# Retention and feed-forward on one core: q and k loads ahead of the weights on GpSimd, then on SyncE; v loaded as stacked fp32 on SyncE; transposes one unit ahead; 256-token groups at both ends

## The chip, the core and the metric

The kernel runs on one core of one Trainium2 chip. A core has five engines, each with its own instruction queue worked in order: TensorE (PE in the profile, with its weight loads as PEld), VectorE (DVE), ScalarE (ACT), GpSimd (POOL) and SyncE (SP, which here only issues DMAs). Sixteen DMA engines move data between memory and the core; SP, ACT and POOL each feed them through a queue of their own. The metric is the device time of one execution in microseconds, lower is better.

## What is computed

q, k and v have the shape (8 batches, 8 heads, 576 positions, 64). The first half is a decaying, causal linear attention (retention), the second a feed-forward with a leaky ReLU over all 4608 tokens, 512 wide with 2048 hidden.

```python
scores = scale * np.matmul(q, k.transpose(0, 1, 3, 2))
gamma = 1.0 - 2.0 ** (-5.0 - np.arange(H))
Dmat = np.where(rel >= 0, gamma[:, None, None] ** rel, 0.0)
attn = np.matmul(scores * Dmat, v)
x = attn.transpose(0, 2, 1, 3).reshape(B * S, H * D)
h = x @ w_in
out = np.maximum(0.01 * h, h) @ w_out
```

## The kernel before

**Units.** The attention is worked in 40 units: each of the 8 batches has four units of 128 tokens and one, the fifth (`w == 4`), of 64. A unit consists of blocks of 64 tokens. For a unit `u` these steps are written:

- `load(u)` (L127): two DMAs on SyncE bring q and k of the unit as fp32, in pieces of 64 numbers (256 bytes), into a pool of four buffers each (`ld`).
- `load_v(b)` (L110): eight DMAs on GpSimd bring v of a whole batch and turn it to fp16 on the way. Two batches have room.
- `cast(u)` (L142): multiplies q and k by the decay tables and makes them fp16 (`qk16`). q is done on GpSimd, k on VectorE for the first five units and on GpSimd later.
- `st_transpose(u)`: VectorE copies v into block-diagonal weights `vdiag` (L162, two copies) and k into `kstk` (L170, four copies of 64x256; none for the unit of 64 tokens); TensorE makes eight transposes (L177) into the PSUM tile `tr`; ScalarE copies `qT` out of it (L184), and ScalarE and VectorE copy half of `kdiag` each (L186).
- `st_state(u, j)`: four matmuls (L203) add a block's k·v to the running state `ups`; VectorE turns it into fp16 weights `sdiag` (L229 to L233).
- `st_scores(u)`: eight matmuls (L242), then VectorE multiplies by the causal mask (L253).
- `st_out(u)`: matmuls with `vdiag` and `sdiag` (L275, L280) into `ot`; ScalarE copies the result to `xT` (L286), the input of the feed-forward.

**Feed-forward.** 4608 tokens are 9 groups of 512. `g1(g, fc)` is four matmuls of 512 columns with `w_in` (L352) into one of two PSUM buffers `hps`, and the leaky ReLU on ScalarE (L359) into `gt`. `g2(g, n)` is four matmuls with `w_out` (L371) into `yps`; every fourth is followed by a copy on VectorE (L380) and the output DMA on SyncE (L382).

**Order.** Nothing is rescheduled: each engine's queue holds its instructions in the order in which the Python code writes them. The attention of a unit is a list of slots: `s0` (load of unit u+4, `load_v` of the next batch when `w == 1`, `cast(u+2)`, `st_transpose(u)`), then state, scores, state, out. The units of the first 512 tokens (0 to 3) are written first. Then, in loop `g`, the 16 pieces of `g1(g)` alternate with the 16 of `g2(g-1)`, and the attention slots of the next group are spread between them evenly, the last one behind the last piece. Loop 8 and the last `g2` hold no attention.

**Start.** SyncE issues q and k of units 0 to 3. GpSimd issues v of batch 0 (eight DMAs), casts q of units 0 and 1, then issues the weights: four DMAs for `w_in` (L325), each a quarter of the hidden columns, and four for `w_out` (L330), all turned to fp16 on the way.

**Waits of the DMA queues.** Eight semaphores serve GpSimd's DMAs in turn and eight others SyncE's. A DMA that takes a semaphore waits until the DMA eight before it has landed. A load into a pool buffer also waits until the engine that read the buffer's last content is done.

Of the kernel before, what the change touches and what calls it, by code (L numbers as in the profile page):

```python
# [18 lines left out]
def kernel(  # L19
# [20 lines left out]
    P = 128  # L40
# [28 lines left out]
    v_pool = ctx.enter_context(tc.tile_pool(name="vp", bufs=2))  # L69
    a_pool = ctx.enter_context(tc.tile_pool(name="ap", bufs=3))  # L70
# [32 lines left out]
    vst = {}  # L103

    def load_v(b):
        t = v_pool.tile([P, NP, NI, D], F16, name="vst")
        vst[b] = t
        for p in range(NP):
            for hh in range(2):
                nc.gpsimd.dma_start(  # L110
                    out=t[CH * hh : CH * hh + CH, p, :, :],
                    in_=v[b, 2 * p + hh].rearrange("(i s) d -> s i d", s=CH),
                )

# [4 lines left out]
    qk16 = {}  # L119

    def load(u):
        b, w = units[u]
        n = nrows[u]
        for x, t_ap in enumerate((q, k)):
            t = ld_pool.tile([P, H, D], FP, name=f"qk32_{x}")
            qk32[u, x] = t
            nc.sync.dma_start(  # L127
                out=t[0:n],
                in_=t_ap[b, :, P * w : P * w + n, :].rearrange("h t d -> t h d"),
            )  # L130

    def cast(u):
        b, w = units[u]
        n = nrows[u]
        for x in range(2):
# [5 lines left out]
            eng = nc.vector if (u < 5 and x == 1) else nc.gpsimd  # L141
# [5 lines left out]
            )  # L147

# [7 lines left out]
    def st_transpose(u):  # L156
# [4 lines left out]
        for hh in range(2):  # L161
            nc.vector.tensor_copy(  # L162
                out=vdiags[z][CH * hh : CH * hh + CH, :, 0:nb, CH * hh : CH * hh + CH],
                in_=vst[b][CH * hh : CH * hh + CH, :, 2 * w : 2 * w + nb, :],
            )
# [19 lines left out]
        for hh, eng in ((0, nc.scalar.copy), (1, nc.vector.tensor_copy)):  # L185
# [7 lines left out]
    def st_state(u, j):  # L193
# [8 lines left out]
        for p in range(NP):  # L202
# [3 lines left out]
                rhs=vst[b][:, p, i, :],  # L206
# [18 lines left out]
        for hh in range(2):  # L225
# [4 lines left out]
            elif nxt < 3:  # L230
                nc.vector.tensor_copy(out=dst, in_=ut[lo:hi])
# [55 lines left out]

    def slots(u):

        b, w = units[u]  # L290

        def s0():
            if u + 4 < NU:
                load(u + 4)
            if w == 1 and b + 1 < B:
                load_v(b + 1)
            if u + 2 < NU:
                cast(u + 2)
            st_transpose(u)

        yield s0
# [15 lines left out]
    load(0)  # L317
    load_v(0)
    for u in range(1, 4):
        load(u)  # L320
    cast(0)
    cast(1)
# [12 lines left out]
    first_slot = []  # L335
    need = []
    for u in range(NU):
        b, w = units[u]
        lo = b * NI + 2 * w
        for s in slots(u):  # L340
            first_slot.append(s)
            need.append(lo // 8)
    done = 0

    g_tiles = {}

    def g1(g, fc):
        if fc == 0:
            g_tiles[g] = g_pool.tile([P, NF, TOK], F16, name="gt")
        hps = h_pool.tile([P, TOK], FP, name="hps")  # L350
        for c in range(NP):
            nc.tensor.matmul(  # L352
                out=hps,
                lhsT=w_in16[:, c, fc * P : (fc + 1) * P],
                rhs=xT[:, c, g * TOK : (g + 1) * TOK],
                start=(c == 0),
                stop=(c == NP - 1),
            )
        nc.scalar.activation(  # L359
            out=g_tiles[g][:, fc, :], in_=hps,  # L360
            func=mybir.ActivationFunctionType.Lrelu,
        )

    y_cur = {}

    def g2(g, n):
        tb, part = n // 4, n % 4
        if part == 0:
            y_cur[g] = y_pool.tile([P, DM], FP, name="yps")
        for f in range(4 * part, 4 * part + 4):  # L370
            nc.tensor.matmul(  # L371
                out=y_cur[g],
                lhsT=g_tiles[g][:, f, tb * P : (tb + 1) * P],
                rhs=w_out16[:, f, :],
                start=(f == 0),
                stop=(f == NF - 1),
            )
        if part == 3:
            osb = o_pool.tile([P, DM], FP, name="osb")
            nc.vector.tensor_copy(out=osb, in_=y_cur[g])  # L380
            r0 = g * TOK + tb * P
            nc.sync.dma_start(out=out[r0 : r0 + P, :], in_=osb)  # L382

    def run_slots(upto):
        nonlocal done
        while done < upto:
            first_slot[done]()
            done += 1

    total = len(first_slot)  # L390
    ends = [sum(1 for x in need if x <= g) for g in range(NG)] + [total]
    run_slots(ends[0])
    for g in range(NG + 1):
        a = done
        e = ends[min(g + 1, NG)] if g < NG else total
        nblk = (16 if g < NG else 0) + (16 if g > 0 else 0)
        m = 0
        for n in range(NF):
            if g < NG:
                g1(g, n)  # L400
                m += 1
                run_slots(a + (e - a) * m // nblk)
            if g > 0:
                g2(g - 1, n)
                m += 1
                run_slots(a + (e - a) * m // nblk)
# [30 lines left out]
```

## Time and profile before

| what | value |
|---|---|
| median of 3 runs | 366.31 us (366.26 to 366.71) |
| the profiled execution | 366.62 us, of which 364.9 us are the span of the trace |
| granted TensorE clock, mean | 0.994 |
| busy: DVE, ACT, POOL | 198.1, 144.2, 131.4 us |
| DMA, whole span | 37.71 MB in 122479 packets, 113744 of them under 512 B |
| issue to landing, median: q or k of 256 KB; v of 72 KB; `w_in`; `w_out` | 4.3 and 4.4; 5.0; 12.5; 23.3 us |

The page divides the span into 40 slices of 9.1 us and shows in each, in tenths, how busy an engine was. Groups of instructions are listed by line, engine and the tiles they write and read, with count, total busy time, mean duration, and the idle time ahead of them with what ended it. The span begins with the first instruction; 1.7 us of the execution's time (366.62 less 364.9) lie around it.

### The profile page before, as it was taken

The numbers are of one execution on the slowest core, as the hardware profiler recorded it, in microseconds if no ns is written. First come the engines' busy times: TensorE is split into PE (matmuls) and PEld (weight loads), VectorE is DVE, ScalarE is ACT, GpSimd is POOL, SyncE is SP. The second block draws the span as 40 slices with busy tenths as digits, with TensorE's granted clock in tenths as the row PEclk, the third lists the DMA queues.
The fourth block names the chain that finished last, engine by engine and source line by source line (L and its number), as shares of the span: only waits on it lengthen the run. The fifth ranks groups of instructions, "written<-read, shape, count | busy, mean of one in ns | idle before, by whom it ended". The sixth has DMA issues, their size and how long they took to land.

```text
span 364.9 us, 6523 instructions
## 1 busy us (share of the span) xinstructions
PE 311.6 (85%) x2560; PEld 168.9 (46%) x2560; DVE 198.1 (54%) x492; ACT 144.2 (40%) x266; POOL 131.4 (36%) x153
## 2 busy tenths in 40 slices
PE   0024278779999999999999999999999999999995
PEld 0023144445554555555555555555555455544442
DVE  5448248782656577636756775445884556300021
ACT  1111046354444455434444444444445444433300
POOL 9822379426322573166225822373132100000000
PEclk9999999899999999999999999999999999999999
DMA  9999999709335393387338943593452000011012
GB/s 158 189 196 196 176 192 182 126 3 78 91 78 128 90 189 89 88 118 93 86 88 156 125 103 77 129 152 88 105 113 73 31 29 32 29 44 44 29 62 84
DMA packets 122479, 37.71 MB, mean 103 GB/s; under 512 B 113744, under 2 KB 117840, under 8 KB 122448
## 3 DMA queue, kind: packets, MB, share of 16 engines
q1 hardware_dynamic: 80192, 28.32, 35.2%
q0 software_dynamic: 42112, 8.92, 27.3%
q8 instruction: 20, 0.33, 0.4%
q10 hardware_dynamic: 144, 0.06, 0.1%
q14 instruction: 11, 0.09, 0.1%
HBM read 36.76 MB, written 9.44 MB: 127 GB/s over the span
## 4 chain that ended last, share of the span: by engine, by line
PE 78%; DMA 7%; DVE 6%; POOL 4%; ACT 2%; issue 2%; POOLq 0%; DVEq 0%
PE yps L371 34%; PE hps L352 32%; DMA w_out<-in_moe_w_out_dram 7%; PE tr L177 4%; PE ot L275 2%; PE sc L242 2%; PE ot L280 2%; POOL vst L110 2%; PE ups L203 2%; ACT xT L286 1%; DVE kstk L170 1%; POOL qk L142 1%; POOL w_in L325 1%; DVE s L253 1%; DVE sdiag L233 1%
## 5 line engine op out<-in xcount | busy, mean ns | idle before, releaser
L352 PE MATMUL hps<-xT,w_in 128*128 128x512 f16 x576 | 149.9, 383 | 5.9 <-ACT xT L286 5.9
L371 PE MATMUL yps<-w_out,gt 128*128 128x512 f16 x576 | 145.2, 379 | 0.0
L359 ACT ACTIVATE gt<-hps 128x512 f16<-128x512 f32 x144 | 86.0, 597 | 133.0 <-PE hps L352 131.8
L142 POOL TENSOR_TENSOR qk<-qk,cs 128x512 f16<-128x512 f32 x60 | 62.5, 1059 | 117.0 <-DMA qk<-in_q_dram 39.5
L371 PEld LDWEIGHTS <-gt 128*128 128x128 f16 x576 | 52.8, 98 | 54.6
L352 PEld LDWEIGHTS <-w_in 128*128 128x128 f16 x576 | 51.0, 99 | 51.7 <-issue 8.1
L110 POOL DMA_DIRECT2D vst<-in_v_dram x64 | 47.5, 775 | 32.8 <-DMA w_out<-in_moe_w_out_dram 11.4
L380 DVE COPY osb<-yps 128x512 f32<-128x512 f32 x36 | 24.9, 691 | 51.3 <-PE yps L371 51.0
L186 DVE COPY kdiag<-tr 64x512 f16<-64x512 f16 (+1 forms) x40 | 16.0, 401 | 59.5 <-ACT kdiag L186 59.2
L286 ACT CAST xT<-ot 128x512 f16<-128x512 f32 (+1 forms) x40 | 21.6, 541 | 40.9 <-PE ot L280 40.9
L203 PE MATMUL ups<-vst,kstk 128*128 128x64 f16 x256 | 18.9, 199 | 21.1 <-DVE kstk L170 11.7
L170 DVE COPY kstk<-qk 64x256 f16<-64x256 f16 x128 | 34.2, 267 | 3.0
L177 PE MATMUL tr<-ident,qk 128*128 128x128 f16 x256 | 21.5, 232 | 15.8 <-POOL qk L142 15.8
L203 PEld LDWEIGHTS <-kstk 128*128 128x128 f16 x256 | 16.4, 102 | 35.6 <-DVE kstk L170 22.2
L184 ACT COPY qT<-tr 128x512 f16<-128x512 f16 (+1 forms) x40 | 21.6, 540 | 27.6 <-PE tr L177 27.6
L233 DVE TENSOR_TENSOR sdiag<-ups,sinit 64x256 f16<-64x256 f32 x64 | 26.9, 421 | 4.2 <-PE ups L203 3.3
L177 PEld LDWEIGHTS <-qk 128*128 128x128 f16 x256 | 18.2, 104 | 22.3 <-POOL qk L142 15.9
L162 DVE COPY vdiag<-vst 64x512 f16<-64x512 f16 (+1 forms) x80 | 27.0, 337 | 1.5
L253 DVE TENSOR_TENSOR s<-sc,cs 128x512 f16<-128x512 f32 x32 | 22.1, 691 | 9.0 <-PE sc L242 8.4
L275 PE MATMUL ot<-s,vdiag 128*128 128x64 f16 x288 | 23.0, 199 | 2.6 <-DVE s L253 2.6
L275 PEld LDWEIGHTS <-vdiag 128*128 128x128 f16 x288 | 20.9, 102 | 5.6 <-issue 1.0
L280 PE MATMUL ot<-qT,sdiag 128*128 128x64 f16 x256 | 22.0, 200 | 0.0
(30 smaller groups left out, 154.0 us busy)
## 6 DMA issues: line engine op xcount, KB each, us to landing
out_dram<-osb SPq DMA_DIRECT2D x36, 256.0 KB, 2.2
qk<-in_q_dram SPq DMA_DIRECT2D x32, 256.0 KB, 4.3
qk<-in_k_dram SPq DMA_DIRECT2D x32, 256.0 KB, 4.4
vst<-in_v_dram POOLq DMA_DIRECT2D x64, 72.0 KB, 5.0
w_in<-in_moe_w_in_dram POOLq DMA_DIRECT2D x4, 512.0 KB, 12.5
w_out<-in_moe_w_out_dram POOLq DMA_DIRECT2D x4, 512.0 KB, 23.3
qk<-in_q_dram SPq DMA_DIRECT2D x8, 128.0 KB, 4.7
qk<-in_k_dram SPq DMA_DIRECT2D x8, 128.0 KB, 4.4
```

The lines of the kernel that those rows point to most:

```text
L110: nc.gpsimd.dma_start(out=t[CH * hh : CH * hh + CH, p, :, :], in_=v[b, 2 * p + hh].rearrange("(i s) d -> s i d", s=CH),)
L142: eng.tensor_tensor(out=t[0:n], in0=qk32[u, x][0:n], in1=tab_sb[0:n, w % 3, x, :].unsqueeze(2).to_broadcast([n, H, D]), op=MUL,)
L162: nc.vector.tensor_copy(out=vdiags[z][CH * hh : CH * hh + CH, :, 0:nb, CH * hh : CH * hh + CH], in_=vst[b][CH * hh : CH * hh + CH, :, 2 * ...
L170: nc.vector.tensor_copy(out=kstks[z][CH * hh : CH * hh + CH, :, j, CH * hh : CH * hh + CH], in_=k16[CH * j : CH * j + CH, :, hh, :],)
L177: nc.tensor.transpose(tr[:, x, p, :], qk16[u, x][:, 2 * p : 2 * p + 2, :].rearrange("t h d -> t (h d)"), ident,)
L203: nc.tensor.matmul(out=ut[:, p, :], lhsT=kstks[z][:, p, j, :], rhs=vst[b][:, p, i, :], start=(i % 3 == 0 and p == 0), stop=(i % 3 == 2), s ...
L233: nc.vector.tensor_tensor(out=dst, in0=ut[lo:hi], in1=sins[b][lo:hi], op=ADD)
L275: nc.tensor.matmul(out=o, lhsT=vdiags[z][:, p, j, :], rhs=s16s[u][:, p, j, :], start=True, stop=(i == 0),)
L280: nc.tensor.matmul(out=o, lhsT=sdiag_at[b, i][:, p, :], rhs=qTs[u][:, p, CH * j : CH * j + CH], start=False, stop=True,)
L352: nc.tensor.matmul(out=hps, lhsT=w_in16[:, c, fc * P : (fc + 1) * P], rhs=xT[:, c, g * TOK : (g + 1) * TOK], start=(c == 0), stop=(c == NP ...
L359: nc.scalar.activation(out=g_tiles[g][:, fc, :], in_=hps, func=mybir.ActivationFunctionType.Lrelu,)
L371: nc.tensor.matmul(out=y_cur[g], lhsT=g_tiles[g][:, f, tb * P : (tb + 1) * P], rhs=w_out16[:, f, :], start=(f == 0), stop=(f == NF - 1),)
```

## The change

- q and k of units 0 to 3 are loaded by GpSimd, ahead of the weights in its queue; all later ones by SyncE as before.
- v is no longer loaded by batch with a conversion on GpSimd. SyncE loads it by unit, as fp32, in two DMAs for each block of 64 tokens (four for a full unit), into a pool of four buffers (`v32`); ScalarE makes it fp16 (`vst`, a third copy in `cast`).
- k is cast on VectorE for all units; q on VectorE for units 0 and 1, on GpSimd later.
- The four `kstk` copies go from VectorE to ScalarE (units 0 to 3) or GpSimd (the rest). ScalarE takes the second half of `kdiag` for units 0 and 1, and the first half of `sdiag` where no earlier state is added.
- `prepare(u+1)` (loads of q and k for u+5 and of v for u+4, transposes of u+1, casts of u+2) stands behind `st_scores(u)`, one unit ahead of where the transposes stood.
- The groups are 4 of 256 tokens, 6 of 512 and 2 of 256. In a group of 256 a PSUM buffer `hps` holds two pieces of 256 columns, so a block is eight matmuls of 256 columns and one leaky ReLU. `g1` of groups 0 and 1 run one after the other; then `g2` of both, two token blocks side by side; then `g1(2)` alone; then `g1(g)` with `g2(g-1)`.
- The attention steps of a run are finished three blocks before its end.

```diff
-                nc.gpsimd.dma_start(
-                    out=t[CH * hh : CH * hh + CH, p, :, :],
-                    in_=v[b, 2 * p + hh].rearrange("(i s) d -> s i d", s=CH),
...
-            nc.sync.dma_start(
+            (nc.gpsimd if u < 4 else nc.sync).dma_start(
                 out=t[0:n],
                 in_=t_ap[b, :, P * w : P * w + n, :].rearrange("h t d -> t h d"),
...
+    def load_v(u):
+        b, w = units[u]
+        t = ld_pool.tile([P, NP, 2, D], FP, name="v32")
+        v32[u] = t
+        for j in range(nrows[u] // CH):
+            t0 = P * w + CH * j
+            for hh in range(2):
+                nc.sync.dma_start(
+                    out=t[CH * hh : CH * hh + CH, :, j, :],
+                    in_=v[b, :, t0 : t0 + CH, :].rearrange(
+                        "(p h) s d -> h s p d", h=2
+                    )[hh],
+                )
...
-            eng = nc.vector if (u < 5 and x == 1) else nc.gpsimd
+            eng = nc.gpsimd if (u >= 2 and x == 0) else nc.vector
...
+        t = a_pool.tile([P, NP, 2, D], F16, name="vst")
+        vst[u] = t
+        nc.scalar.copy(out=t[:, :, 0:nb, :], in_=v32[u][:, :, 0:nb, :])
...
-                    nc.vector.tensor_copy(
+                    (nc.scalar.copy if u < 4 else nc.gpsimd.tensor_copy)(
                         out=kstks[z][CH * hh : CH * hh + CH, :, j, CH * hh : CH * hh + CH],
...
+    def prepare(u):
+        if u == 4:
+            cast(4)
+        if u + 4 < NU:
+            load_qk(u + 4)
+        if 4 <= u + 3 < NU:
+            load_v(u + 3)
+        st_transpose(u)
+        if u + 1 < NU and u != 3:
+            cast(u + 1)
...
         yield lambda: st_state(u, 0)
         yield lambda: st_scores(u)
+        if u + 1 < NU:
+            yield lambda: prepare(u + 1)
...
-    load(0)
-    load_v(0)
-    for u in range(1, 4):
-        load(u)
+    for u in range(4):
+        load_qk(u)
+        load_v(u)
     cast(0)
-    cast(1)
...
+    sizes = [256] * 4 + [512] * 6 + [256, 256]
...
+            run_steps(min(upto, a + -(-(upto - a) * (m + 1) // max(1, len(order) - 3))))
+
+    run_steps(ends[0])
+    run(ends[1], g1_blocks(0))
+    run(ends[1], g1_blocks(1))
+    run(ends[2], g2_blocks(0, 2) + g2_blocks(1, 2))
+    run(ends[3], g1_blocks(2))
+    for g in range(3, NG):
+        run(ends[g + 1], g1_blocks(g), g2_blocks(g - 1))
+    run(ends[NG], g2_blocks(NG - 1))
```

Three places of the instruction order matter below. The first is the start of GpSimd's queue. Before (`DMASW0` to `DMASW7` are the eight semaphores of its DMAs; `qk_0` is q, `qk_1` k, fp32 on the right of the arrow):

```order
L110 DMA vst<-in_v_dram 64x9x64 x8
L142 TENSOR_TENSOR qk_0_150<-qk_0_125,cs 128x512 [waits DMAHW1_49,DMAHW0_49]
L142 TENSOR_TENSOR qk_0_154<-qk_0_138,cs 128x512 [waits DMAHW3_49]
L325 DMA w_in_101<-in_moe_w_in_dram 128x4x512 [waits DMASW0_49]
...
L330 DMA w_out_102<-in_moe_w_out_dram 128x4x512 [waits DMASW7_49]
L142 TENSOR_TENSOR qk_0_170<-qk_0_142,cs 128x512 [waits DMAHW5_49]
L110 DMA vst<-in_v_dram 64x9x64 [waits DMASW0_49]
L110 DMA vst<-in_v_dram 64x9x64 [waits DMASW1_49]
```

And now, with q of unit 2 as `qk_0_140`, of unit 3 as `qk_0_149`:

```order
L116 DMA qk_0_149<-in_q_dram 128x8x64
L116 DMA qk_1_151<-in_k_dram 128x8x64
L336 DMA w_in_98<-in_moe_w_in_dram 128x4x512 [waits DMASW0_49]
...
L341 DMA w_out_99<-in_moe_w_out_dram 128x4x512 [waits DMASW7_49]
L147 TENSOR_TENSOR qk_0_245<-qk_0_140,cs 128x512 [waits DMAHW0_49]
L147 TENSOR_TENSOR qk_0_318<-qk_0_149,cs 128x512
L147 TENSOR_TENSOR half_109<-qk_0_172,cs 64x512 [waits DMAHW1_49,DVE_49]
```

The eight v loads of batch 1 that stood between the weights and the later casts are gone; the last weight DMA now waits for k of unit 3, the eighth DMA of the queue, and the cast of unit 2's q stands behind it.

The second is SyncE's queue after the change, from the loads of unit 4 on (`qk_0_172` is q of unit 4, 219 of unit 5, 290 of unit 6; `v_223` is v of unit 4, `v_294` of unit 5). Before, only q and k loads stood here.

```order
L116 DMA qk_0_219<-in_q_dram 128x8x64 [waits DMAHW3_49,DMASW2_49,DVE_49]
L116 DMA qk_1_221<-in_k_dram 128x8x64 [waits DMAHW4_49,DMASW3_49,DVE_49]
L128 DMA v_223<-in_v_dram 64x4x64 [waits DMAHW5_49,Activation_49]
L128 DMA v_223<-in_v_dram 64x4x64 [waits DMAHW6_49]
L116 DMA qk_0_290<-in_q_dram 128x8x64 [waits DMAHW7_49,DMASW4_49,Pool_49]
L116 DMA qk_1_292<-in_k_dram 128x8x64 [waits DMAHW0_49,DMASW5_49,DVE_49]
L128 DMA v_294<-in_v_dram 64x4x64 [waits DMAHW1_49,Activation_49]
```

v of unit 5 stands behind q and k of unit 6, and q of unit 6 waits for GpSimd (it reuses the buffer whose q GpSimd casts for unit 2).

The third is ScalarE's queue in the run of `g1(0)`. Before, with the first pieces of `g1(0)` as `ACTIVATE`:

```order
L359 ACTIVATE gt<-hps 128x512 [waits PE_49]
L184 COPY qT<-tr 128x4x64 [waits PE_49]
L186 COPY kdiag_103<-tr 64x4x64 [waits Activation_49]
L359 ACTIVATE gt<-hps 128x512 [waits PE_49] x2
L286 CAST xT<-ot 128x4x64 [waits PE_49]
```

Now, from the fourth of the eight blocks of `g1(0)` (`gt_349`) to those of `g1(1)` (`gt_579`):

```order
L389 ACTIVATE gt_349<-hps 128x512 [waits PE_49]
L155 CAST vst<-v_223 128x4x64 [waits DMAHW6_49,DMAHW5_49]
L192 COPY qT<-tr 128x4x64 [waits PE_49]
L195 COPY kdiag_100<-tr 64x4x64 [waits Activation_49]
L155 CAST vst<-v_294 128x512 [waits DMAHW3_49,DMAHW4_49,DMAHW2_49,DMAHW1_49]
L389 ACTIVATE gt_349<-hps 128x512 [waits PE_49]
L295 CAST xT<-ot 128x4x128 [waits PE_49]
L389 ACTIVATE gt_349<-hps 128x512 [waits PE_49] x3
L389 ACTIVATE gt_579<-hps 128x512 [waits PE_49] x8
```

The conversion of unit 5's v, which waits for four DMAs, now stands between the fourth and the fifth leaky ReLU of that run.

More of the change, by code (lines that the diff above doesn't have):

```diff
@@ L119, with load_qk @@
     qk16 = {}
-    def load(u):
+    v32 = {}
+    vst = {}
+    def load_qk(u):
         b, w = units[u]
@@ L333 @@
         )
-    first_slot = []
+    sizes = [256] * 4 + [512] * 6 + [256, 256]
+    starts = [sum(sizes[:g]) for g in range(len(sizes))]
+    NG = len(sizes)
+    steps = []
     need = []
@@ L338 @@
         b, w = units[u]
-        lo = b * NI + 2 * w
+        lo = b * S + P * w
         for s in slots(u):
-            first_slot.append(s)
-            need.append(lo // 8)
+            steps.append(s)
+            need.append(max(g for g in range(NG) if starts[g] <= lo))
+    ends = [sum(1 for x in need if x <= g) for g in range(NG)]
+    ends += [ends[-1]] * 2
     done = 0
[L345 to L382, printed above, removed]
@@ L384, in run_slots, with run_steps @@
-    def run_slots(upto):
+    def run_steps(upto):
         nonlocal done
         while done < upto:
-            first_slot[done]()
+            steps[done]()
             done += 1
[L390 to L393, printed above, removed]
-        a = done
[L395 to L406, printed above, removed]
+    g_tiles = {}
```

87 lines of the change are left out of this document (64 added, 23 removed).

## Prediction

> **What bounds the kernel now.** I read the page's busy shares and slices first, then a table of stages, then the queues in the first 50 us.
>
> ```profile
> PE 311.6 (85%) x2560; PEld 168.9 (46%) x2560; DVE 198.1 (54%) x492; ACT 144.2 (40%) x266; POOL 131.4 (36%) x153
> PE   0024278779999999999999999999999999999995
> 0.00:50.54 50.54, 12.78 (x157) 10.32 (x157) 26.76 (x69) 7.90 (x14) 28.05 (x39) 1.00 1.36 183
> 114.69:319.38 204.69, 200.06 (x1708) 108.39 (x1708) 124.99 (x316) 94.12 (x177) 70.98 (x78) 1.00 0.54 96
> ```
>
> The stage rows give start and end, length, busy time of PE, PEld, DVE, ACT and POOL, then clock and DMA. From slice 11 on PE is full: loops 2 to 7 (114.69 to 319.38) are 200.06 busy of 204.69. The first 50.54 us hold 12.78. So there are two kinds of time to win: the start, and little in the loops. The start, from the timeline (start, duration, instruction, in brackets the wait ahead of it):
>
> ```profile
> 18.31 0.80 POOL L110 DMA_DIRECT2D vst<-in_v_dram  x1 [1.53 <-DMA w_in<-in_moe_w_in_dram]
> ...
> 31.72 0.73 POOL L110 DMA_DIRECT2D vst<-in_v_dram  x1 [2.55 <-DMA w_out<-in_moe_w_out_dram]
> ...
> 42.72 0.73 POOL L110 DMA_DIRECT2D vst<-in_v_dram  x1 [2.84 <-DMA w_out<-in_moe_w_out_dram]
> 43.47 1.05 POOL L142 TENSOR_TENSOR qk<-qk,cs 128x512 f16<-128x512 f32 x1
> 44.58 1.03 PE L177 MATMUL tr<-ident,qk 128*128 128x128 f16 x8 [7.18 <-POOL qk L142]
> 50.54 1.87 PE L352 MATMUL hps<-xT,w_in 128*128 128x512 f16 x4 [0.67 <-ACT xT L286]
> ```
>
> Each v load of batch 1 waits for one weight DMA to land, so these eight rows are also the landing times of the weights: `w_in` from 18.3, `w_out` from 31.7 to 42.7. The cast of unit 3's q stands behind them and starts at 43.47; only then come its transposes, its output and the first feed-forward matmul at 50.54, although `w_in` had long been there. GpSimd's queue order holds the start, not the bytes.
>
> What is left for PE after that moment is nearly incompressible:
>
> ```profile
> 346.14 14.84 PE L371 MATMUL yps<-w_out,gt 128*128 128x512 f16 x68
> 60.61 1.03 PE L352 MATMUL hps<-xT,w_in 128*128 128x512 f16 x4
> PE hps L352 <- ACT xT L286: 5.9, 9, 0.7
> 361.02 0.69 DVE L380 COPY osb<-yps 128x512 f32<-128x512 f32 x1 [2.76 <-PE yps L371]
> ```
>
> 68 matmuls of 512 columns in 14.7 us (the last ends at about 361.0; the modelled 14.84 holds its drain) are 0.216 us each; 1152 of them are 248.8 us. Loops 2 to 7 took 204.69, of which 6 x 128 x 0.216 = 165.9 are feed-forward; 38.8 remain, 6.47 per 512 tokens, for attention with its stalls. Of this 0.66 is the wait in the third row (5.9 us in 9 times, total first, then count): the first `g1` of each loop waits for the `xT` copy of the attention step that ended the loop before. PE ends at 361.0; the copy, the last output DMA and the close make the span 364.9, so the tail is 3.9, and 1.7 lie around it (366.62).
>
> **The change part by part.**
>
> *New order of the first transfers.* The eight v loads of batch 1 leave GpSimd, and q and k of units 0 to 3 pass ahead of the weights in its queue. The rates, from the DMA view of three stretches (total, or one queue; q0 is GpSimd's, q1 SyncE's; packets, MB, share):
>
> ```profile
> DMA packets 4846, 0.91 MB, mean 182 GB/s; under 512 B 4846, under 2 KB 4846, under 8 KB 4846
> ...
> q0 software_dynamic: 1589, 1.58, 91.8%
> q1 hardware_dynamic: 1588, 0.40, 29.9%
> 28.56 6.40 SPq L127 DMA_DIRECT2D qk<-in_q_dram  x1
> ```
>
> The first row is 5 to 10 us: small packets of 256 bytes from both queues, 969 per us. The next two are 18.3 to 28.4 us, the weights against q and k: the queues got 1589 and 1588 packets in 10.1 us, so they alternate one for one, and SyncE's queue moves only 157 packets per us, while a weight packet is large. The last row shows it from SyncE's side: one load of 1024 packets kept it 6.4 us.
>
> After the change the weights start when q and k of units 0 to 3 (8192 packets) are through. Beside them go v of units 0 to 3 (4096), q, k of units 4 and 5 (3072) and v of unit 4 (512): 15,872 packets at 969 per us are 16.4 us, and packets began to flow at about 1.8 us (the 0 to 5 us row below has its first non-zero tenth there). So the weights start at 18.2. Neither q nor k on GpSimd is in the trace; the bounds:
>
> ```profile
> GB/s 0 0 0 0 0 0 0 0 0 0 0 0 0 0 59 97 177 131 87 160 212 260 289 291 287 289 287 287 266 268 268 236 240 209 195 180 172 162 175 192
> q0 software_dynamic: 42112, 8.92, 27.3%
> L110 POOL DMA_DIRECT2D vst<-in_v_dram x64 | 47.5, 775 | 32.8 <-DMA w_out<-in_moe_w_out_dram 11.4
> ```
>
> At the best rate seen, 287 GB/s or 1121 packets per us, it is 16.0. At GpSimd's mean packet time over the whole run (27.3% of 364.9 us on 16 engines over 42112 packets, 37.8 ns, the large weight packets included) and 14.3 ns for SyncE's (16 engines at 1121 per us), it is 1.8 + 19.4 + 6.9 = 28.1. I take 18.2, as 969 is the same mixture. An issue costs GpSimd 0.775 us in the last row (576 pieces), for 1024 pieces in proportion 1.4: eight take 11 us, less than the transfers.
>
> *What is late next: v of unit 5.* The last `w_out` DMA waits for k of unit 3, 18.2 plus a landing delay of 1.3 (an output DMA of the same size lands in 2.2 us on the page, less 0.9 for its bytes): 19.5. Its issue takes 0.76 and the cast of unit 2's q 1.05; SyncE then issues q of unit 6 at about 21.7. Behind it are k of unit 6 and v of unit 5, 3072 packets, now against the weights: at 157 per us 19.6 us, and 1.3 to land, 42.6. In ScalarE's queue the conversion of this v stands ahead of the fifth leaky ReLU of `g1(0)`. PE may fill the two `hps` buffers (blocks five and six) and then waits for ScalarE. Until then it has the time it needs: `w_in` arrives in quarters at 3.36 us (before: 18.31 to 31.72 in four steps), so at about 23, 26, 29.6 and 33, and blocks one to six need three quarters. Conversion 0.54 and leaky ReLU 0.60 (rows below) later, at 43.7, PE goes on.
>
> ```profile
> L359 ACT ACTIVATE gt<-hps 128x512 f16<-128x512 f32 x144 | 86.0, 597 | 133.0 <-PE hps L352 131.8
> L184 ACT COPY qT<-tr 128x512 f16<-128x512 f16 (+1 forms) x40 | 21.6, 540 | 27.6 <-PE tr L177 27.6
> ```
>
> *What is left then.* Feed-forward: 248.8 less six blocks of 0.86 = 243.6. Attention of tokens 512 to 4607: eight times 5.8 = 46.4, where 5.8 is 6.47 less 0.66, since all steps of a run now end three blocks (2.6 us) before its end, longer than the wait that goes.
>
> *Cold clock.* PE will have been idle for some 10 us. The four matmuls at 50.54 took 1.87 against about 0.86 (1.03 with the drain) at 60.61. I charge two blocks at half speed, 1.7 us; nothing to 3.4 (four blocks) are the bounds.
>
> *Groups of 256.* 384 matmuls of 256 columns replace 192 of 512. Columns stay; the fixed part of a matmul and its weight load count. Eight score matmuls of 64 columns lie within 0.41 us in the row below, at most 0.05 each, so a load of 128 columns can't cost more than that: 192 x 0.05 = 9.6 is the upper bound, nothing the lower; I take 0.5, as the loads at full width hide today behind matmuls of 64 columns.
>
> ```profile
> 58.66 0.41 PE L242 MATMUL sc<-qT,kdiag 128*128 128x64 f16 x8 [0.67 <-DVE kdiag L186]
> ```
>
> At the end of the kernel PE is already full (26.93 of 26.93 in loop 8), so groups of 256 there win and cost nothing more.
>
> *Work moved between engines.* The rows are group totals and mean ns:
>
> ```profile
> L162 DVE COPY vdiag<-vst 64x512 f16<-64x512 f16 x64 | 22.9, 358 | 1.1
> L142 DVE TENSOR_TENSOR qk<-qk,cs 128x512 f16<-128x512 f32 x4 | 3.2, 812 | 12.4 <-DMA qk<-in_k_dram 12.4
> L186 DVE COPY kdiag<-tr 64x512 f16<-64x512 f16 x32 | 13.7, 427 | 39.5 <-ACT kdiag L186 39.2
> L233 DVE TENSOR_TENSOR sdiag<-ups,sinit 64x256 f16<-64x256 f32 x64 | 26.9, 421 | 4.2 <-PE ups L203 3.3
> L253 DVE TENSOR_TENSOR s<-sc,cs 128x512 f16<-128x512 f32 x32 | 22.1, 691 | 9.0 <-PE sc L242 8.4
> L142 POOL TENSOR_TENSOR qk<-qk,cs 128x512 f16<-128x512 f32 x60 | 62.5, 1059 | 117.0 <-DMA qk<-in_q_dram 39.5
> 60.99 2.34 DVE L162 COPY vdiag<-vst 64x512 f16<-64x512 f16 x2
> ```
>
> VectorE per full unit afterwards: 2 x 0.358 + 0.812 + 0.427 + 4 x 0.421 + 0.691 = 4.3 us. A unit lasts 204.69 / (6 x 4.44) = 7.7 us in the loops, so it hides. GpSimd: one cast of 1.06 and four copies of half its elements, not in the trace; 0.2 (its `ident` memset) to 1.06 each, I take 0.5: 3.1 us, at most 5.3, hidden too. ScalarE: four copies of 0.54 and 3.6 leaky ReLUs of 0.60, 4.3 us. Only the run of `g1(2)` is too short: five blocks and two units' matmuls, 5 x 0.86 + 2 x 1.31 = 6.9, against 8.6 of VectorE: 1.7 us of stall.
> The Trainium skill, "GPSIMD Engine Reference", section "4.1 Engine selection", advises against elementwise work on GpSimd, and section "1. Specifications" says that its SBUF interfaces are shared with VectorE. The last row agrees with the sharing: two copies took 2.34 us instead of 0.72 while GpSimd cast. With a collision of that size in every unit VectorE would need 5.9 us, still under 7.7; from what size on it decides is the last rival.
>
> **Sum.** 43.7 + 243.6 + 46.4 + 1.7 + 0.5 + 1.7 = 337.6; tail 3.9: span 341.5; around it 1.7: **343.2 us**, against 366.62 of the profiled execution, which is 0.3 above the median; I say 343.
>
> **Rivals.**
> - *v of unit 5 doesn't gate* (it gets more than every second packet, or is early): PE then goes on with the last quarter of `w_in` at 33, 10.7 sooner, and doesn't cool, 1.7: 331. For it: small packets alone run seven times as fast. Against it: 1589 to 1588, and the place of q of unit 6 behind GpSimd's cast. The Trainium skill, "DMA: Bandwidth & Descriptors", section "Queues, rings and completion order", has an engine drain a packet of some 9 to 17 descriptors before it changes queues; by that, bursts of small pieces would bring v of unit 5 early, which is this rival. The rows do not bear it out: 0.40 MB in 1588 packets are 252 bytes each, single pieces that alternate with single weight packets.
> - *q and k on GpSimd are slow.* The weights start at 28.1 instead of 18.2, all behind it shifts: 353. For it: GpSimd's packets have the longer mean; against it: the 969.
> - *The wait at the loops' ends stays* and only changes its place: 8 x 0.66 = 5.3 more, 348. That would be the change not doing what it says in the loops.
> - *Slower than before: VectorE becomes the bound.* In loops of units, if collisions with GpSimd's four new copies bring VectorE's chain per unit above the 7.7 us that PE needs. The gain of 23 us is gone at 7.7 + 23/36 = 8.3 us per unit over 36 units; at twice the sum of the rows, 8.7, the time is 343 + 36 x 1.0 = 379. For it: vdiag at 2.34. Against it: even this gives 5.9, and GpSimd loses its 47.5 us of v issues.
>
> **How the numbers follow.** The forecast with its small terms (337 to 347) 0.60; no gate 0.10; slow q and k 0.17; the wait stays 0.06; slower 0.05; no difference 0.02. The range leaves out the gate case, the upper part of the slow case and the last two: 334 to 354. About 0.2%, 0.7 us, is what a measurement of this kernel can tell from none; faster by more 0.93, within 0.02, slower 0.05.
>
> **What would show it.** Weights landing from about 23 to 46; ScalarE idle for about 10 us before the conversion of unit 5's v near 42.6; PE without work from the middle thirties to 43.7; no wait for `xT` at the loops' starts; loops of 33.4 us for 512 tokens; GpSimd's copies near 0.5 us. Wrong it would be if the first feed-forward matmul came later than 30 us, if PE waited in the loops for `kstk` or VectorE, or if ScalarE did not wait for v.

## The result, and the profile after

| kernel | median | range | ratio to before (95% interval) |
|---|---|---|---|
| before (in the same comparison) | 366.28 us | 365.96 to 366.71 | 1 |
| after | 354.55 us | 353.95 to 354.86 | 0.9677 (0.9659 to 0.9695) |

The change wins 11.7 us; 23 were forecast, and 354.55 lies just above the range. The profiled execution took 354.83 us, its span is 353.1. The page of the kernel after, with busy shares, slices of 8.8 us, the SP and POOL DMA queues (q1 and q0: packets, MB, share of the engines' time) and one group:

```profile
PE 309.0 (88%) x2752; PEld 186.2 (53%) x2752; DVE 176.6 (50%) x383; ACT 173.1 (49%) x340; POOL 97.7 (28%) x172
PE   1336429988988998999999999999999999999995
PEclk9999968999999999999999999999999999999999
q1 hardware_dynamic: 111040, 35.67, 43.9%
q0 software_dynamic: 4864, 6.29, 9.8%
L178 POOL COPY kstk<-qk 64x256 f16<-64x256 f16 x112 | 44.4, 397 | 161.3 <-DVE qk L147 100.9
```

PE begins the feed-forward in the fourth slice (6 tenths), but the fifth and sixth hold 4 and 2: it starts and stops. Of slices 9 to 16 (70.6 to 141 us) five show an 8. So there are two losses, one at the start and one in the short runs. The start, from the timelines of ScalarE and PE (start, duration, instruction, in brackets the wait ahead of it):

```profile
28.48 0.62 ACT L155 CAST vst<-v 128x512 f16<-128x512 f32 x1 [2.51 <-DMA v<-in_v_dram]
...
38.69 0.60 ACT L389 ACTIVATE gt<-hps 128x512 f16<-128x512 f32 x1 [1.19 <-PE hps L382]
45.69 0.40 ACT L155 CAST vst<-v 128x256 f16<-128x256 f32 x1 [6.40 <-DMA v<-in_v_dram]
46.26 0.36 ACT L195 COPY kdiag<-tr 64x256 f16<-64x256 f16 x1
49.34 0.62 ACT L155 CAST vst<-v 128x512 f16<-128x512 f32 x1 [2.72 <-DMA v<-in_v_dram]
49.87 0.59 ACT L389 ACTIVATE gt<-hps 128x512 f16<-128x512 f32 x1
```

```profile
29.63 1.86 PE L382 MATMUL hps<-xT,w_in 128*128 128x256 f16 x8 [3.14 <-ACT xT L295]
...
42.50 1.04 PE L382 MATMUL hps<-xT,w_in 128*128 128x256 f16 x8
50.51 11.75 PE L382 MATMUL hps<-xT,w_in 128*128 128x256 f16 x80 [6.97 <-ACT gt L389]
```

The fourth leaky ReLU (38.69) is followed by the conversions of v of units 4 and 5, which wait for their DMAs; the fifth comes at 49.87. PE filled the two `hps` buffers (the sixth block at 42.50) and stood for 6.97 us, from 43.54 to 50.51. Both conversions count: that of unit 4's v, which the forecast had landed with the first transfers, came only at 45.69 and with the two copies behind it held ScalarE until 46.62, over the first 3.1 us of PE's gap; that of unit 5's v held it over the rest. The stages (start and end, length, busy time of PE, PEld, DVE, ACT, POOL, then clock, DMA share, GB/s):

```profile
29.63:50.51 20.88, 9.85 (x128) 8.31 (x128) 8.27 (x20) 8.67 (x18) 4.48 (x7) 0.90 1.10 195
62.00:100.00 38.00, 35.28 (x401) 24.74 (x399) 26.12 (x55) 20.20 (x43) 13.92 (x26) 1.00 0.57 131
100.00:150.00 50.00, 46.04 (x474) 27.95 (x473) 37.51 (x80) 29.36 (x61) 18.94 (x36) 1.00 0.65 146
150.00:200.00 50.00, 50.00 (x440) 27.32 (x437) 27.26 (x60) 28.60 (x57) 16.44 (x31) 1.00 0.55 127
```

From 62 to 150 us PE is idle for 2.7 + 4.0 = 6.7 us, from 150 to 200, the last row, for none. In 100 to 150 VectorE is busier than behind it (37.51 of 50 against 27.26).

**Where v of unit 5 lost its time.** SyncE's queue (issue start and length), and the DMA view of four stretches (10 to 15, 20 to 40, 40 to 45 us, then 0 to 18.2):

```profile
0.74 15.36 SPq L128 DMA_DIRECT2D v<-in_v_dram  x16
...
25.09 6.45 SPq L116 DMA_DIRECT2D qk<-in_k_dram  x1
31.64 8.42 SPq L128 DMA_DIRECT2D v<-in_v_dram  x2
40.16 0.55 SPq L116 DMA_DIRECT2D qk<-in_q_dram  x1
...
44.04 2.86 SPq L128 DMA_DIRECT2D v<-in_v_dram  x4
```

```profile
DMA packets 1024, 1.04 MB, mean 208 GB/s; under 512 B 815, under 2 KB 815, under 8 KB 1024
q0 software_dynamic: 257, 0.86, 83.0%
q1 hardware_dynamic: 767, 0.19, 27.6%
...
q0 software_dynamic: 3148, 3.13, 91.9%
q1 hardware_dynamic: 3145, 0.78, 29.9%
...
q1 hardware_dynamic: 2684, 0.67, 72.9%
q0 software_dynamic: 395, 0.39, 45.6%
...
q0 software_dynamic: 1028, 2.49, 66.7%
q1 hardware_dynamic: 3076, 0.74, 27.0%
```

In 10 to 15 us, 209 packets (1024 less 815) are over 2 KB, all of them GpSimd's, and carry nearly all of its 0.86 MB: 4.1 KB each, as much as 16 pieces of 256 bytes. q and k on GpSimd, which are not converted on the way, travel in bundles; SyncE's v travels in single pieces (0.19 MB in 767) and gets 153 of them per us, three packets for one of GpSimd's (767 to 257). The forecast had 7680 packets of SyncE through by 18.2 us; there were 3076, and v of unit 4 was not among them. What was left then crept against the weights (3145 to 3148 in 20 us, the 157 per us of the forecast) until the weights ended soon after 40; in 40 to 45 us SyncE's queue moved 537 per us. Ahead of 18.2 us the queue had fallen too far behind for that to save units 4 and 5.

### The profile page after: what moved, and what is told of

Its sections match the earlier page's. It is cut to its first block, busy times and chain, and to the rows that moved or that the text cites. A ratio compares the mean times of both kernels' runs of the same rounds, so it can differ in the third digit from the quotient of the medians.

```text
span 353.1 us, 7062 instructions
## 1 busy us (share of the span) xinstructions
PE 309.0 (88%) x2752; PEld 186.2 (53%) x2752; DVE 176.6 (50%) x383; ACT 173.1 (49%) x340; POOL 97.7 (28%) x172
## 4 chain that ended last, share of the span: by engine, by line
PE 74%; DMA 9%; DVE 5%; SPq 4%; ACT 3%; issue 3%; POOL 2%; ACTq 0%; POOLq 0%; DVEq 0%
PE hps L382 33%; PE yps L405 31%; DMA v<-in_v_dram 7%; PE tr L185 4%; SPq L128 3%; PE sc L251 2%; PE ups L212 2%; PE ot L284 2%; PE ot L289 1%; DVE qk L147 1%; SPq L116 1%; POOL kstk L178 1%; DVE osb L415 1%; DMA qk<-in_q_dram 1%; DMA qk<-in_k_dram 1%
## 5 line engine op out<-in xcount | busy, mean ns | idle before, releaser
L382 PE MATMUL hps<-xT,w_in 128*128 128x256 f16 (+1 forms) x768 | 150.1, 333 | 10.1 <-ACT gt L389 7.0
L382 PEld LDWEIGHTS <-w_in 128*128 128x128 f16 x768 | 72.3, 100 | 51.7 <-issue 10.4
L178 POOL COPY kstk<-qk 64x256 f16<-64x256 f16 x112 | 44.4, 397 | 161.3 <-DVE qk L147 100.9
L405 PEld LDWEIGHTS <-gt 128*128 128x128 f16 x576 | 51.9, 98 | 47.7 <-issue 0.4
L147 POOL TENSOR_TENSOR qk<-qk,cs 128x512 f16<-128x512 f32 x30 | 31.3, 1046 | 11.1 <-DMA qk<-in_q_dram 9.4
L212 PEld LDWEIGHTS <-kstk 128*128 128x128 f16 x256 | 16.2, 100 | 29.1 <-issue 16.4
L155 ACT CAST vst<-v 128x512 f16<-128x512 f32 (+1 forms) x40 | 23.1, 578 | 15.2 <-DMA v<-in_v_dram 15.2
L147 DVE TENSOR_TENSOR qk<-qk,cs 128x512 f16<-128x512 f32 x34 | 23.4, 692 | 2.2 <-DMA qk<-in_k_dram 0.8
L284 PE MATMUL ot<-s,vdiag 128*128 128x64 f16 x288 | 21.9, 196 | 1.3 <-DVE s L262 1.3
L195 ACT COPY kdiag<-tr 64x512 f16<-64x512 f16 (+1 forms) x42 | 22.7, 540 | 0.1
```

What stands on the lines that cost most here:

```text
L147: eng.tensor_tensor(out=t[0:n], in0=qk32[u, x][0:n], in1=tab_sb[0:n, w % 3, x, :].unsqueeze(2).to_broadcast([n, H, D]), op=MUL,)
L178: (nc.scalar.copy if u < 4 else nc.gpsimd.tensor_copy)(out=kstks[z][CH * hh : CH * hh + CH, :, j, CH * hh : CH * hh + CH], in_=k16[CH * j ...
L195: eng(out=kdiags[z][CH * hh : CH * hh + CH, :, 0:nb, CH * hh : CH * hh + CH], in_=tr[CH * hh : CH * hh + CH, 1, :, 0:n].rearrange("e p (j ...
L212: nc.tensor.matmul(out=ut[:, p, :], lhsT=kstks[z][:, p, j, :], rhs=vst[u][:, p, j, :], start=(i % 3 == 0 and p == 0), stop=(i % 3 == 2), s ...
L284: nc.tensor.matmul(out=o, lhsT=vdiags[z][:, p, j, :], rhs=s16s[u][:, p, j, :], start=True, stop=(i == 0),)
L382: nc.tensor.matmul(out=hps[:, f, :], lhsT=w_in16[:, c, fc * P : (fc + 1) * P], rhs=xT[:, c, t0 : t0 + tok], start=(c == 0), stop=(c == NP ...
```

## The experiments

All edits are against the kernel after (354.55 us, 0.9677). Each ratio is to the kernel before, timed again beside the run (365.58 to 366.59 us).

**Is it the conversion's place in ScalarE's queue?** `vst_pool`: v of units 4 and 5 is converted on GpSimd.

```diff
-        nc.scalar.copy(out=t[:, :, 0:nb, :], in_=v32[u][:, :, 0:nb, :])
+        (nc.gpsimd.tensor_copy if u in (4, 5) else nc.scalar.copy)(
+            out=t[:, :, 0:nb, :], in_=v32[u][:, :, 0:nb, :]
+        )
```

> The conversion of v of units 4 and 5 is done on GpSimd instead of ScalarE; nothing else. Queue theory (PE waits only because two conversions stand in ScalarE's queue ahead of leaky ReLUs that have their data): PE's wait of 7.0 us ahead of 50.5 us goes, and most of the cold blocks behind it; time 345 to 347 us. Data theory (the next attention step needs this v anyway): PE waits for it a little later instead, time 353 to 354.6 us.

345.32 us, 0.942 (0.9397 to 0.9442): 9.2 us faster, as the queue theory had it. PE's timeline, then GpSimd's:

```profile
40.94 1.04 PE L384 MATMUL hps<-xT,w_in 128*128 128x256 f16 x8
42.40 9.77 PE L384 MATMUL hps<-xT,w_in 128*128 128x256 f16 x88
```

```profile
45.20 0.40 POOL L155 CAST vst<-v 128x256 f16<-128x256 f32 x1 [12.95 <-PE hps L384]
...
49.26 0.61 POOL L155 CAST vst<-v 128x512 f16<-128x512 f32 x1 [2.66 <-DMA v<-in_v_dram]
```

v of units 4 and 5 comes as late as in the kernel after, at 45.20 and 49.26, and PE waits for neither: the bytes were not needed yet, only the instructions stood in the way. The 88 matmuls take 0.111 us each, so PE doesn't go cold either. The gap of 7 us and the cold clock behind it were the price of the place of these two instructions.

**Is it the large packets?** `qk_conv`: q and k of units 0 to 3 are converted to fp16 by their DMAs (and so rounded ahead of the decay), so that GpSimd's packets become single pieces.

```diff
             t = ld_pool.tile([P, H, D], FP, name=f"qk32_{x}")
+            if u < 4:
+                t = t[:, :, :].bitcast(F16)[:, :, 0:D]
```

> q and k of units 0 to 3 are turned to fp16 by the DMA on GpSimd (v was so before), all else as in the changed kernel; q and k are rounded to fp16 once more. Packet theory (GpSimd's unconverted pieces travel in packets of 2.7 KB, 2.1 MB in 768 packets, the queues alternate by packets, so SyncE's pieces of 256 bytes are held back from the first us on): converted pieces travel singly, SyncE gets over 400 packets per us between 5 and 15 us instead of 153 to 216, v of unit 3 is converted by ScalarE at about 16 us instead of 28.5, that of unit 5 at about 43 instead of 49.3, time about 348 us. Issue theory (SyncE's sixteen small v loads are held up by their own issue and semaphores): v of unit 3 stays near 28, time within 1 us of 354.6.

352.33 us, 0.9612 (0.959 to 0.9634). The DMA view of 5 to 15 us:

```profile
DMA packets 9700, 1.60 MB, mean 160 GB/s; under 512 B 9629, under 2 KB 9700, under 8 KB 9700
q0 software_dynamic: 6954, 0.94, 139.3%
q1 hardware_dynamic: 2746, 0.66, 45.4%
```

GpSimd's packets are single pieces now (in the kernel after they are 4.1 KB, not the 2.7 KB of the expectation: by 18.2 us 512 packets over 2 KB carry the 2.1 MB), and SyncE's rate goes from 185 per us (the kernel after, same stretch) to 275. The packets' size does matter: v of unit 3 is converted at 21.51 instead of 28.48. But 275 is not the 400 expected, and v of unit 5 is converted only at 47.77 instead of 49.34: behind unit 3 the weights take over, and the rest goes at their pace whatever came first.

So the bundles are only a part of what the forecast missed. Of the 7680 packets that it had through by 18.2 us there are now 4090 instead of 3076 (first row below). The two queues together move 970 per us, just the 969 of the forecast, but they don't share them evenly (6954 to 2746). In the kernel before they did (second and third row, 5 to 10 us):

```profile
q1 hardware_dynamic: 4090, 0.99, 35.7%
...
q0 software_dynamic: 2463, 0.31, 95.9%
q1 hardware_dynamic: 2383, 0.60, 78.8%
...
0.74 11.27 SPq L130 DMA_DIRECT2D v<-in_v_dram  x16
```

There a load on SyncE had 1024 pieces; now v comes in loads of 256, and sixteen of them keep SyncE for 11.27 us even here (last row, `qk_conv`). The forecast priced GpSimd's issues but not SyncE's. How much of the uneven share is due to them, these runs don't settle.

**Would v be better on GpSimd?** `v_gpsimd`: v of units 0 to 3 is issued by GpSimd too, behind q and k of each unit.

```diff
-                nc.sync.dma_start(
+                (nc.gpsimd if u < 4 else nc.sync).dma_start(
                     out=t[CH * hh : CH * hh + CH, :, j, :],
```

> v of units 0 to 3 is issued by GpSimd, unit by unit behind q and k, instead of SyncE. Packet theory: v travels in large packets too, that of unit 3 lands at about 17 us, the first loads of SyncE (unit 4) start at about 8 us, v of unit 5 lands at 43 to 46 us, time 349 to 351 us. Issue theory: sixteen more issues of 0.7 us on GpSimd put the weights off by 11 us, time 355 or more.

355.89 us, 0.971 (0.9687 to 0.9733): nothing won, as the issue theory had it. v of unit 3 is converted at 30.64, of unit 5 at 50.83. GpSimd's 16 more issues push its casts of q back (the casts of units 2 and 3 to 27.34); the conversion of unit 3's v now stands behind these casts and not behind its DMA, and SyncE waits for them until 28.46 before q of unit 6. That is the gate that the forecast had in the kernel after; there the casts start at 17.80, long before SyncE's queue comes to q of unit 6 at 40.16.

**Is it SyncE's backlog?** `six_qk`: q and k of units 0 to 5 go on GpSimd ahead of the weights, with six buffers and loads two units earlier; v of units 4 and 5 then follows v of unit 3 directly on SyncE.

```diff
-    ld_pool = ctx.enter_context(tc.tile_pool(name="ld", bufs=4))
+    ld_pool = ctx.enter_context(tc.tile_pool(name="ld", bufs=6))
...
-            (nc.gpsimd if u < 4 else nc.sync).dma_start(
+            (nc.gpsimd if u < 6 else nc.sync).dma_start(
...
-        if u + 4 < NU:
-            load_qk(u + 4)
-        if 4 <= u + 3 < NU:
-            load_v(u + 3)
+        if u + 6 < NU:
+            load_qk(u + 6)
+        if 6 <= u + 5 < NU:
+            load_v(u + 5)
...
-    for u in range(4):
+    for u in range(6):
```

> q and k of units 0 to 5 (not 0 to 3) go through GpSimd ahead of the weights, with six load buffers instead of four; v stays on SyncE, in the order of units, so v of units 4 and 5 no longer stands behind q and k of units 4 to 6. Starvation theory (the start is set by how few of SyncE's small pieces get through beside GpSimd's queue, about 185 per us, 157 beside the weights): v of units 0 to 5 are 5632 pieces, landed at about 31 us instead of 49.3; PE goes on at about 36 us with the last quarter of w_in instead of 50.5; time 338 to 342 us. Byte theory (all first transfers together fill the DMA engines, so what comes earlier pushes something else back by as much): the weights land 6 us later and the time stays above 348 us.

347.31 us, 0.9505 (0.9475 to 0.9536), between the two expectations. The gate is gone (ScalarE's and PE's timelines: the conversion of unit 5 waits for no DMA, and PE works on from 44.48 without a gap), but v of unit 3 is converted only at 30.45 and the feed-forward begins at 31.61, 2 us later than in the kernel after (with six units on GpSimd it begins at 31.05 to 31.61 in three runs; in `vst_pool`, `both` and `kcast_pool`, with four, at 27.41 to 29.66): the start pays for four more bundled loads ahead of the weights.

```profile
43.75 0.62 ACT L155 CAST vst<-v 128x512 f16<-128x512 f32 x1
44.27 0.59 ACT L389 ACTIVATE gt<-hps 128x512 f16<-128x512 f32 x1
```

**Is the idle time in the short runs VectorE's?** `kcast_pool`: k from unit 6 on is cast on GpSimd again, nearly as before the change (there from unit 5 on).

```diff
-            eng = nc.gpsimd if (u >= 2 and x == 0) else nc.vector
+            eng = nc.gpsimd if (u >= 2 and x == 0) or u >= 6 else nc.vector
```

> k of units 6 and later is cast on GpSimd again instead of VectorE. VectorE theory (PE's idle time between 62 and 150 us, 6.7 us in the changed kernel, comes from VectorE's full queue in the short runs): 0.69 us less per unit there takes half of it away, about 351 us. Rival (it is the latency of transposes, ScalarE, VectorE that a short run can't hide, and GpSimd's kstk copies then start later behind its second cast): time 354 or more, new waits of PE for kstk.

349.24 us, 0.9547 (0.9525 to 0.9568): 5.3 us faster (4.8 by the ratios), where about 3.5 were expected. The same stages as above, PE first:

```profile
62.00:100.00 38.00, 36.52 (x421) 25.68 (x419) 23.31 (x54) 21.21 (x44) 20.86 (x34) 1.00 0.60 138
100.00:150.00 50.00, 49.13 (x490) 29.31 (x488) 31.29 (x70) 30.94 (x63) 28.95 (x45) 1.00 0.66 151
```

PE is idle for 2.4 us instead of 6.7 between 62 and 150, which is most of the gain, and VectorE's load from 100 to 150 falls from 37.51 to 31.29. The PE timeline of the kernel after shows what stood there: each of the three stalls below waits for work at the end of VectorE's chain (half of `kdiag`, cast of k, then `stmp` or `sdiag`), or for `kstk`, which GpSimd copies from the cast k.

```profile
86.72 0.28 PE L212 MATMUL ups<-vst,kstk 128*128 128x64 f16 x4 [1.36 <-DVE stmp L231]
102.05 0.28 PE L212 MATMUL ups<-vst,kstk 128*128 128x64 f16 x4 [1.21 <-POOL kstk L178]
107.50 0.28 PE L212 MATMUL ups<-vst,kstk 128*128 128x64 f16 x4 [1.31 <-DVE sdiag L242]
```

**Does the margin of three blocks win what the wait cost?** `no_margin`: the steps of a run end with the run.

```diff
-            run_steps(min(upto, a + -(-(upto - a) * (m + 1) // max(1, len(order) - 3))))
+            run_steps(min(upto, a + -(-(upto - a) * (m + 1) // max(1, len(order)))))
```

> The attention steps of a run end with its last block again, not three blocks earlier. Margin theory: the wait of 0.66 us for xT at each run's start is back in eight to ten runs, 354.6 + 5.3 = about 360 us. Rival: the wait was only shifted to other places by the margin; time within 1 us of 354.6.

352.38 us, 0.9611 (0.958 to 0.9643): not slower but 2 us faster. The wait for `xT` is back, as its row in the table of waits says (total, times, longest):

```profile
PE hps L382 <- ACT xT L295: 14.6, 6, 8.7
```

The longest stands at the start, in the place of the wait for v; the other five are 5.9 us. But between 62 and 150 PE is idle for 4.7 us instead of 6.7, and the start differs too. So the margin wins no time here; that it is the steps squeezed into fewer blocks that cost it is argued, not shown.

**What are the groups of 256 worth?** `all512`: nine groups of 512, the runs in the plain order. `end512`: only the two at the end become one of 512.

```diff
 all512
-    sizes = [256] * 4 + [512] * 6 + [256, 256]
+    sizes = [512] * 9
...
-    run(ends[1], g1_blocks(1))
-    run(ends[2], g2_blocks(0, 2) + g2_blocks(1, 2))
-    run(ends[3], g1_blocks(2))
-    for g in range(3, NG):
+    for g in range(1, NG):
 end512
-    sizes = [256] * 4 + [512] * 6 + [256, 256]
+    sizes = [256] * 4 + [512] * 7
```

> Nine groups of 512 tokens instead of 4 of 256, 6 of 512 and 2 of 256; g1(0) alone, then g1(g) with g2(g-1). My theory: the first feed-forward matmul comes behind v of unit 5, at about 50 us as in the kernel before; the six blocks that the changed kernel does before that (5.2 us) are lost, and the idle time of the short runs between 62 and 150 us (6.7 us) goes for the most part: 353 to 356 us. If the groups of 256 are what brings the gain: 360 or more.

> The last 512 tokens are one group of 512 instead of two of 256. Theory: PE is full at the end either way, 354.5 within 0.7 us. Rival: shorter last groups save drain or cost weight loads: a change of over 1 us.

`all512`: 356.98 us, 0.9755 (0.973 to 0.978), 2.4 us slower than after and 1 us above the expected range. Its first feed-forward matmul starts at 50.34, as late as PE goes on in the kernel after: here the first `xT` copy stands behind the same two conversions. So the small groups won the six blocks that PE does ahead of its gap (5.2 us by the forecast's 0.86 each) and gave most of it back in the short runs, where `all512` is idle for 1.7 us instead of 6.7; `all512` then loses 2.4 us between 50.51 and 62, where PE is busy for 9.10 of 11.49 us and in the kernel after for all of it. `end512`: 353.96 us, 0.9678 (0.9661 to 0.9694): the small groups at the end do nothing.

**Together.** `both` has the edits of `vst_pool` and `kcast_pool`; `both_conv` has those and `qk_conv`'s; `six_kc` is `six_qk` with `kcast_pool`; `six_kc_nm` is `six_kc` with `no_margin`.

> Conversion of v of units 4 and 5 on GpSimd, and k cast on GpSimd from unit 6 on, together. If the wait in ScalarE's queue (9.2 us alone) and VectorE's full queue in the short runs (5.3 us alone) are two separate costs: 354.55 - 9.2 - 5.3 = 340, say 339 to 342. Rival: the gap in ScalarE's queue gone, the short runs start while VectorE is still behind, so the two overlap: 342 to 345. Rival two: GpSimd with both jobs becomes late itself and PE waits for kstk: above 345.

> The same two edits and q, k of units 0 to 3 converted on the way, so that they travel in single pieces. Alone that gave 2.2 us, by an earlier start of the state matmuls, while the goings-on of v of unit 5 stayed. If the start before the first feed-forward matmul still counts when ScalarE no longer waits: 337 to 339. Rival: the weights, issued later behind more packets of q and k, now hold PE: 340 or more, with PE waiting for w_in or w_out.

> Six units of q and k on GpSimd and k cast on GpSimd from unit 6 on. If the short runs are VectorE's alone: 347.3 - 5.3 = 342, say 341 to 343.5. Rival: with two more units prepared ahead the short runs wait less for VectorE already: 345 to 347.

> As the last, but the attention steps of a run end with the run, not three blocks before. If the margin cost its 2.2 us by crowding VectorE, it should cost nothing once VectorE is relieved, and without it the wait for xT at the loops' starts (5.9 us in 5) counts: 3 to 6 us slower than the last. Rival: crowding is of PE's order itself, not of VectorE's load: 1 to 2 us faster than the last.

| kernel | median | ratio to before (95% interval) |
|---|---|---|
| `both` | 340.19 us | 0.9286 (0.9261 to 0.931) |
| `both_conv` | 338.71 us | 0.9239 (0.9217 to 0.9261) |
| `six_kc` | 343.11 us | 0.9359 (0.9339 to 0.9378) |
| `six_kc_nm` | 343.44 us | 0.9369 (0.9345 to 0.9393) |

`both` comes out at the sum of its parts (354.55 less 9.2 and 5.3 is 340.0): two separate costs. `both_conv` is the best of all, 1.5 us below, though not by what its start wins: PE's unbroken run of `g1` begins at 36.09 instead of 40.43, and then two rows show the next wait, PE's and ScalarE's:

```profile
55.57 0.28 PE L216 MATMUL ups<-vst,kstk 128*128 128x64 f16 x4 [2.45 <-DVE sdiag L244]
```

```profile
53.91 0.62 ACT L157 CAST vst<-v 128x512 f16<-128x512 f32 x1 [4.66 <-DMA v<-in_v_dram]
```

ScalarE again stands before a conversion, now of unit 6's v, and what follows in its queue is `xT`; from 51 to 57 PE is busy for 3 of 6 us. From 57 to 60 us the granted clock is 0.50 again. It is the same mechanism one unit on, which the expectation had not named (its rival spoke of `w_in` and `w_out`). That the conversion of unit 6 on GpSimd too would win these 3 us was not tried.

`six_kc` lies in its range. `six_kc_nm` is the same within the intervals, where 3 to 6 us more were expected: with k's casts off VectorE the margin neither wins nor loses. PE's waits for `xT` in `six_kc_nm` are 5.9 us in 6 against 2.4 in one, but PE does more of its work from 29.63 to 50.51 (16.46 us against 14.99).

## Why the prediction was wrong

Against its own sum (343.2) the profiled execution is 11.6 longer. By its terms: PE goes on at 50.51 instead of 43.7, +6.8; cold clock 2.9 instead of 1.7, +1.2; idle in the short runs 6.7 instead of 1.7, +5.0; the rest together 1.4 better.

- **The step that failed: "15,872 packets at 969 per us are 16.4 us", with SyncE's share of them done by 18.2.** SyncE's queue got 3076 packets through instead of 7680. So v of unit 4, counted among them, was converted only at 45.69, and q of unit 6, which the forecast had issued at 21.7, was issued at 40.16 with v of unit 5 behind it. One part is shown: q and k on GpSimd travel in bundles, and with single pieces (`qk_conv`) SyncE's queue gets 4090 through. The number 969 came from the kernel before, whose GpSimd loads of that stretch were all converted; the rate was carried over to loads of another kind. The other and larger part stays open: with single pieces the rate is 970, but SyncE's queue gets 28% of it, and SyncE's own issues, 11 us for the sixteen v loads, were a term that the forecast put at nothing.
- **The start of the weights.** They did start about when forecast (the last q or k load landed at 17.0, against 18.2), but by other steps, and that is luck: GpSimd's bundles were through while more than half of SyncE's packets were not. The rival in which q and k on GpSimd are slow (353 us) comes close to the time, but its mechanism, weights from 28.1 on, didn't occur.
- **The rule of the Trainium skill**, "DMA: Bandwidth & Descriptors", section "Queues, rings and completion order", that an engine drains a packet of several descriptors before it changes queues, was rejected from rows that held no such load; the 4.1 KB packets of 10 to 15 us agree with it in size. It came out the other way than the rival there said: the bundles were GpSimd's, and made v of unit 5 later, not earlier.
- **v of unit 5, and q of unit 6 behind GpSimd's cast.** The cast was early enough (17.80 instead of 20.3) and gated nothing, as SyncE came to q of unit 6 only at 40.16. Only `v_gpsimd` has that gate. (In the forecast, 19.5, 0.76 and 1.05 add up to 21.3, not 21.7, which changes little.)
- **ScalarE's queue.** The mechanism was right: the conversions stand between the fourth and fifth leaky ReLU, PE fills two buffers and waits, and goes on a moment after the conversion of unit 5's v. `vst_pool` shows the cause directly. What the forecast didn't have is that unit 4's v gates as well: ScalarE waited 6.40 us for it and then 2.72 for unit 5's. The rival in which v doesn't gate came to 331; with the gate taken out the kernel takes 345.32, the short runs and the late start being still there.
- **The two blocks of cold clock** were more: from 50.51 to 56 us the granted clock is 0.50.

```profile
50.51:53.00 2.49, 2.49 (x12) 0.50 0.76 149
53.00:56.00 3.00, 3.00 (x16) 0.50 0.92 199
56.00:59.00 3.00, 3.00 (x28) 0.94 0.55 124
```

  Half of 5.5 us and 6% of three are 2.9; the upper bound of 3.4 held it.
- **VectorE in short runs: 1.7 us of stall in one run of 6.9 us.** The mechanism was right, its size wrong: PE was idle for 6.7 us between 62 and 150. The price was taken from sums of busy time per run, but PE waits for single results in VectorE's in-order queue, in several runs, and `kcast_pool` takes 4.3 us of the idle time away. That moved work hides holds from 150 us on.
- **The margin, 5.3 us of gain.** The waits at the loops' starts vanish as forecast, and no time is won: `no_margin` is 2 us faster than after, `six_kc_nm` equal to `six_kc`. The prediction took a wait that goes for time that goes. What eats the gain stays open: with k's casts off VectorE there is still none.
- **Groups of 256 "win and cost nothing more" at the end**: `end512` agrees. GpSimd's copies took 0.397 us for a taken 0.5, and VectorE as the bound of the whole (379) didn't come: from 150 to 300 us PE is never idle, and the `vdiag` copies, of which two took 2.34 us beside a cast in the kernel before, take 0.363 us each on average against 0.358.

Direction and the kind of gate were right, then; the forecast missed because it took an even share of the packets for SyncE's queue that loads of another kind and size didn't get, and because a stall of a full queue was priced by sums.

## What to carry to other kernels

An instruction that waits for a DMA, put into the queue of the engine that frees PE's output buffers, costs PE all of the DMA's delay that the filled buffers don't cover (here 7.0 us, and a cold clock behind it), though nobody needs the data yet: put such conversions on an engine whose next instructions aren't urgent, and look which unit's load is late next. Before moving small-piece loads to another queue, look for a row with just this kind of load, and in it at the packets' size and at how the queues share: here 1 to 1 beside the weights, 3 to 1 for SyncE beside the bundles, 2 to 5 beside single pieces. Price the issues of many small loads too. A wait removed by doing work earlier is not yet time won: take it out and measure.

## What the runs showed of the hardware

- Loads of 256-byte pieces on GpSimd's queue that change the type go piece by piece (6954 packets for 0.94 MB in `qk_conv`), those that don't go in packets of 4.1 KB, and SyncE's loads beside them move 153 to 216 single pieces per us (5 to 15 us of the kernel after), against 674 in 45 to 50 us when they are alone:

```profile
DMA packets 3373, 0.85 MB, mean 169 GB/s; under 512 B 3372, under 2 KB 3372, under 8 KB 3372
```

- Sixteen loads of 256 pieces each kept SyncE 15.36 us in the kernel after, 11.27 in `qk_conv` and 11.13 in `both_conv`, where GpSimd's pieces are single. None of them took less than 0.595 us, and four take 2.57 us with the weights long through:

```profile
57.61 2.57 SPq L128 DMA_DIRECT2D v<-in_v_dram  x4
```

  So small loads are limited by their issues as well, at about 400 pieces per us by this row. That may be part of why the two queues don't share evenly in `qk_conv`; no run shows it.
- After a gap of 7 us PE ran at a granted clock of 0.50 for 5.5 us of unbroken work.
